# An attention and max-out kernel on one Trainium2 core: 84 steps at which the order of the main part departs from its own rule

## The chip, the core and the metric

The kernel runs on one core of one Trainium2 chip. The metric is the device time in microseconds (us) of one execution. Before the change its median over 10 runs is 330.27 us, from 329.93 to 330.78.

## What is computed

Cut to what matters, the reference is:

```python
# B, N, m, C = 4, 12544, 32, 128; d_ff = 1024
def mab(q, kv):                       # attention in which keys and values are the same rows
    s = (q @ kv.transpose(0, 2, 1)) / sqrt(C)
    a = exp(s - s.max(-1)); a /= a.sum(-1) + 1e-9
    return a @ kv
h = mab(inducing, x)                  # 32 inducing rows look at all of x: "pooling", h is 32 x 128 per batch
y = mab(x, h)                         # every row of x looks at the 32 rows of h
out = maximum(y @ w1, y @ w2) @ w_out # 50176 rows in all
```

The kernel uses max(a, b) = a + relu(b - a). With E the exponentials of the second attention (32 per row), it forms relu(E @ (h @ (w2 - w1))), multiplies it by w_out, adds the linear part E @ (h @ w1 @ w_out), and divides each row by the sum of its exponentials at the very end.

## The kernel before

The 50176 rows are cut into 392 chunks of 128 rows, 98 per batch. Sixteen chunks (four "quarters" of four) make a block. There are three kinds of work for TensorE, and they use the array in three shapes:

- A **phase** (L899, matmuls at L957) works in row tiles: four matmuls, one per quarter, each with 32 rows of the array and 512 output columns, side by side. Each fills one of the eight PSUM banks with the input of a relu. One of the four may be the linear part of a group ("L", four matmuls with 128 columns, written `ps<-m,e`). ScalarE (L973) or VectorE (L976) then evicts each relu bank into the `relu` tile; whichever the planner thinks will end sooner takes it. Every phase needs four free banks.
- A **final product** (L792 in `final_one`, L780) works with the whole array: one chunk's relu piece times one eighth of w_out, 128 columns. There are 3136 of them. Thirty-two make a group of four chunks, which VectorE scales into an output tile (L819 in `evict_group`) and SyncE's queue stores (L844). The sums of exponentials (L622 in `dens`) are small full-array matmuls.
- **Work in column tiles**: staging a block, which makes its E (`stage`, L582, evicted by ScalarE at L594), and, for the pooling of the next batch, its scores (`pool_scores`, L309, evicted at L320) and its accumulation (`pool_accum`, L357 and L370, added up by VectorE at L385). The scores need x transposed by DMA (L171), the accumulation needs the exponentials transposed by DMA (L346); both are issued on SyncE's queue, from `side_work`, by count of chunks done. The next batch's x is loaded by GpSimd's queue (L165) once the last accumulation of a batch has been summed (L391).

The order of the main part is not written out by hand and not left to a scheduler. A loop (L1097) makes it, one step at a time, while the program is built. It keeps a clock, `ck`, with estimates of when TensorE, ScalarE, VectorE and each bank come free. The next four phase jobs have a time `tp` at which the banks and the staged block are ready; the next final product has a time `tf` at which its relu piece is ready. The rule takes the phase if

```python
if tp < INF and lag() <= 128 + LIMIT and (tp <= ck.pe + early or tp <= tf and tf > ck.pe):
    if column_work(len(jobs) + 1):
        continue
    phase(jobs)
```

and otherwise the final product. `lag()` counts how far the phases are ahead. `column_work` looks just before a phase, or when the array is not in its full shape, for work in column tiles whose bank is free; it stages a block that is soon wanted, and it runs a pooling job if the array is already in column tiles, if two or more such jobs wait, or if the job is late. After the last step every engine has a fixed instruction list, with semaphores between engines; nothing is decided at run time.

Of the kernel before, what the change touches and what calls it, by code (L numbers as in the profile page):

```python
# [16 lines left out]
INF = 1e9  # L17
# [85 lines left out]
def kernel(  # L103
# [35 lines left out]
    ck = Clock()  # L139
# [57 lines left out]
    with tc.manual_schedule(engines={ET.PE, ET.DVE, ET.Activation, ET.Pool, ET.SP}):  # L197
# [313 lines left out]
        def weights_1b():  # L511
            for h in range(2):
                nc.gpsimd.tensor_sub(w21[:, 512 * h : 512 * (h + 1)], w_of[h][0], w_of[h][1])
# [16 lines left out]
        def weights_3():  # L530
            bi, ps = bank([128, 512])
            ck.wait(max(ck.bank[bi], w_of["w1T"]), "w")
            for jb in range(NJB):
                nc.tensor.matmul(
                    out=ps[:, 0:128],
                    lhsT=w1T[:, jb, :],
                    rhs=woutp[:, jb, :],
                    start=(jb == 0),
                    stop=(jb == NJB - 1),
                )  # L540
            end = ck.run(0.056 * NJB)
            nc.scalar.mul(out=w1out, in_=ps[:, 0:128], mul=-1.0)
            ck.bank[bi] = w_of["w1out"] = ck.on_act(end, 0.2)
# [303 lines left out]
        def finals_left():  # L847

            n = -state["mm"]
            for i in range(state["g"], state["lin"]):  # L850
                n += len(groups[i].chunks) * NJB
            return n

        def next_job(q):

            k, u = ptr[q]
            while k < len(blocks) and (q >= len(blocks[k].units) or u >= len(blocks[k].units[q])):
                k, u = k + 1, 0
            ptr[q] = [k, u]
            if k >= len(blocks):  # L860
                return None
            blk = blocks[k]
            if blk.staged is None:
                return None
            if relu_slot(blk, q) is None:
                return None
            return blk, blk.units[q][u]

        def want_linear():
            while state["lin"] < len(groups) and groups[state["lin"]].full:  # L870
                state["lin"] += 1
            if state["lin"] >= len(groups):
                return None
            g = groups[state["lin"]]
            if g.blk.staged is None or finals_left() > LINEAR_AHEAD:
                return None
            if st[g.blk.b].get("m1r", 0.0) > ck.pe + 0.2:
                return None
            return g

        LINEAR_AHEAD = 18
        LIMIT = -16

        def plan_phase(linear=True):
            jobs = []
            gl = want_linear() if linear else None
            for q in range(4):
                if gl is not None and gl.chunks[0][0] == q:
                    jobs.append(("L", q, gl, None))
                    continue  # L890
                j = next_job(q)
                if j is not None:
                    jobs.append(("U", q, j[0], j[1]))
            return jobs

        def lag():
            return 4 * state["issued"] - state["done"]
# [116 lines left out]
        def ready(f, a):  # L1014

            d = st[a[0]]
            now = ck.pe
            if f is pool_scores and a[1] >= NEU and ("eT", a[1] - NEU) not in d:
                return False
            if f is pool_turn and a[1] >= NEU and ("sum", a[1] - NEU) not in d:  # L1020
                return False
            if f is pool_scores:
                return d.get(("T", (U * a[1] + U - 1) // (P1 // 2)), INF) + 8.0 <= now
            if f is pool_rest:
                return d.get(("T", 13), INF) + 6.0 <= now
            if f is pool_turn:
                return d.get(("eu", a[1]), (0, INF))[1] <= now
            if f is pool_accum:
                return d.get(("eT", a[1]), (0, INF))[1] + 9.5 <= now and (a[1] < NU - 1 or "et" in d)
            if f is small_rep:  # L1030
                return d.get("esrr", INF) <= now
            if f is small_h:
                return d.get("haccr", INF) <= now
            if f in (small_hwd, small_m1):
                if f is small_m1 and a[0] == 0 and w_of["w1out"] > now:
                    return False
                return d.get("hT4r", INF) <= now
            return True
# [4 lines left out]
        def side_work():  # L1043
            while jobs_at and min(jobs_at) <= chunks_done[0]:
                pending.extend(jobs_at.pop(min(jobs_at)))
            for job in list(pending):
                f, a = job
                if f in COL or not ready(f, a):
                    continue
                if f in FULL:  # L1050
                    if min(ck.bank) > ck.pe + 0.1 or ck.mode != "full":
                        continue
                    pending.remove(job)
                    f(*a)
                    return
                pending.remove(job)
                f(*a)

        def column_work(banks):

            if sorted(ck.bank)[banks - 1] > ck.pe + 0.12:
                return False
            if want_stage(8 if chunks_done[0] > 14 else 3):
                stage(blocks[state["stage"]])
                state["stage"] += 1
                return True
            jobs = [job for job in pending if job[0] in COL and ready(*job)]
            late = jobs and (chunks_done[0] >= due[jobs[0]] + 8 or jobs[0][1][1] == NU - 1)
            if jobs and (ck.mode == "col" or len(jobs) > 1 or late):
                pending.remove(jobs[0])  # L1070
                f, a = jobs[0]
                f(*a)
                return True
            return False

        def want_stage(ahead):
            k0 = state["stage"]
            if k0 >= len(blocks):
                return False
            left = []  # L1080
            for q in range(4):
                next_job(q)
                k, u = ptr[q]
                left.append(sum(len(blk.units[q]) for blk in blocks[k:k0] if q < len(blk.units)) - u)
            free = k0 < NE2 or min(g.blk.index for g in groups[state["g"] :]) > k0 - NE2
            return min(left) <= ahead and free and all(
                "hT4" in st[qu.b] and "hwd" in st[qu.b] for qu in blocks[k0].quarters if qu
            )

        phase(plan_phase(False))  # L1090
        weights_3()
        phase(plan_phase(False))
# [1 line left out]
        state["stage"] = 2  # L1094
        weights_1b()
        START = ck.pe
        while state["g"] < len(groups) or held:  # L1097
            side_work()
            if held and ck.mode == "full":
                linear_last(0.0)  # L1100
            if ck.mode != "full" and column_work(1):
                continue
            if min(ck.bank) <= ck.pe + 0.1 and want_stage(1):
                stage(blocks[state["stage"]])
                state["stage"] += 1
                continue
            jobs = plan_phase()
            tp = INF
            tf = final_ready()
            useful = len(jobs) == 4 or jobs and (tf >= INF or state["stage"] == len(blocks) and lag() <= 48)  # L1110
            if useful and len(jobs) > 0:
                fr = sorted(ck.bank)[len(jobs) - 1]
                tp = max([fr - 0.095] + [(a.blk.staged if kind == "L" else a.staged) for kind, q, a, u in jobs])
            early = 0.2 if ck.mode == "col" else 0.0
            if tp < INF and lag() <= 128 + LIMIT and (tp <= ck.pe + early or tp <= tf and tf > ck.pe):
                if column_work(len(jobs) + 1):
                    continue
                phase(jobs)
            elif tf < INF:
                keep_busy(tf)  # L1120
                ck.wait(tf, "relu")
                final_one()
            elif tp < INF:
                phase(jobs)
            elif pending:
                f, a = pending.pop(0)
                f(*a)
            else:
                raise AssertionError(("stuck", state, ptr, chunks_done, jobs, pending[:3]))
        assert not pending and not jobs_at  # L1130


# [28 lines left out]
```

The softmax here doesn't subtract the row's maximum and nothing guards it: scores larger than these inputs give would overflow.

## Time and profile before

| | before |
|---|---|
| median of 10 runs | 330.27 us |
| the profiled execution | 329.93 us |
| its span, first to last instruction | 328.0 us |
| TensorE busy (PE) | 322.0 us, 98% |
| VectorE busy (DVE) | 285.3 us, 87% |
| ScalarE busy (ACT) | 280.6 us, 86% |
| GpSimd busy (POOL) | 25.8 us, 8% |
| share of TensorE in the chain that ended last | 96% |
| granted TensorE clock | 1.000 |
| DMA, mean over the span | 164 GB/s |

The profile is that of one execution of 329.93 us. Its span is 1.93 us shorter than its time, and the execution is the fastest of the ten, 0.34 us under the median. "Busy" counts an instruction from its start to its end; matmuls overlap, so a final product is shown with 220 ns though one follows the other every 56 ns. The distances between starts are therefore what counts on TensorE. Until about 25 us the kernel pools the first batch; the first final product starts at 25.6 us, the last at 324.4 us, and the stretch between is the main part that the loop orders.

### The profile page before, as it was taken

To read this page: it belongs to the slowest core of one execution; us is meant where nothing else is said; L and a number is where in the kernel's file an instruction comes from. 1 tells how busy PE (TensorE), PEld (TensorE's weight loads), DVE (VectorE), ACT (ScalarE), POOL (GpSimd) and SP (SyncE) were. 2 spreads that over 40 slices of the span, in tenths; PEclk is the share of its full clock that TensorE was granted. 3 is DMA by queue.
4 is the path that set the end of the run, shared out by engine and by line. 5 is a ranking of instruction groups with operands and counts; after the bars stand their busy time and mean duration, and the time that the engine had idled before them with its cause. 6 is when DMAs were issued, how large, how long until landed. Compare 5 with 4: busy or idle time off the path is not lost.

```text
span 328.0 us, 12601 instructions
## 1 busy us (share of the span) xinstructions
PE 322.0 (98%) x5401; PEld 243.7 (74%) x5401; DVE 285.3 (87%) x532; ACT 280.6 (86%) x562; POOL 25.8 (8%) x54
## 2 busy tenths in 40 slices
PE   7999999999999999999999999999999999999996
PEld 3886777777767777777787777777767777778785
DVE  3359999999989999998989999988989989989873
ACT  3689899998789899988888999998968999999961
POOL 7351030000310000000040000000000000000000
PEclk9999999999999999999999999999999999999999
DMA  8999999975299998672379999983212312222233
GB/s 207 207 206 214 285 239 183 194 205 163 58 232 243 238 234 187 171 155 95 125 147 243 232 254 206 194 181 100 103 61 98 114 67 99 98 98 98 82 115 113
DMA packets 70823, 53.65 MB, mean 164 GB/s; under 512 B 52176, under 2 KB 55408, under 8 KB 70768
## 3 DMA queue, kind: packets, MB, share of 16 engines
q1 hardware_dynamic: 64656, 38.63, 47.6%
q0 software_dynamic: 6112, 14.22, 22.1%
q8 instruction: 42, 0.69, 0.9%
q14 instruction: 13, 0.11, 0.1%
HBM read 28.33 MB, written 25.69 MB: 165 GB/s over the span
## 4 chain that ended last, share of the span: by engine, by line
PE 96%; DVE 1%; issue 1%; ACT 0%; DVEq 0%; ACTq 0%
PE ps L792 60%; PE ps L957 22%; PE ps L582 3%; PE ps L232 2%; PE ps L357 1%; PE ps L309 1%; PE ps L648 1%; PE ps L248 1%; PE ps L280 1%; PE ps L622 1%; DVE relu L976 1%; PE ps L749 1%; PE ps L271 1%; PE ps L640 0%; PE ps L464 0%
## 5 line engine op out<-in xcount | busy, mean ns | idle before, releaser
L973 ACT ACTIVATE relu<-ps 128x512 f16<-128x512 f32 x463 | 244.6, 604 | 31.1 <-PE ps L957 24.1
L976 DVE TENSOR_SCALAR relu<-ps 128x512 f16<-128x512 f32 x321 | 205.8, 681 | 18.8 <-PE ps L957 17.9
L792 PE MATMUL ps<-woutp,relu 128*128 128x128 f16 x3136 | 218.1, 220 | 0.0
L792 PEld LDWEIGHTS <-relu 128*128 128x128 f16 x3136 | 177.3, 98 | 39.4 <-issue 28.3
L957 PE MATMUL ps<-e,hwd 32*128 32x512 f16 (+2 forms) x880 | 89.0, 360 | 0.0
L819 DVE TENSOR_TENSOR o<-ps,rp 128x512 f32<-128x512 f32 (+3 forms) x108 | 68.6, 635 | 5.7 <-PE ps L792 3.1
L957 PEld LDWEIGHTS <-hwd 32*128 32x128 f16 x880 | 25.0, 91 | 21.1 <-issue 0.8
L957 PE MATMUL ps<-m,e 32*128 32x128 f16 x381 | 38.8, 217 | 0.0
L957 PEld LDWEIGHTS <-e 32*128 32x128 f16 x381 | 21.4, 92 | 2.6
L165 POOL DMA_DIRECT2D xn<-in_x_dram x31 | 16.8, 552 | 8.1 <-DMA xn<-in_x_dram 4.4
L236 DVE COPY xT<-ps 128x512 f16<-128x512 f16 (+3 forms) x11 | 5.5, 504 | 7.8 <-PE ps L232 7.7
L594 ACT ACTIVATE e<-ps 128x512 f16<-128x512 f32 (+2 forms) x21 | 11.6, 572 | 0.0
L320 ACT ACTIVATE eu<-ps 128x512 f16<-128x512 f32 x18 | 10.8, 619 | 0.0
L582 PE MATMUL ps<-xT,hT 128*32 128x512 f16 (+3 forms) x114 | 10.1, 366 | 0.0
L164 POOL COPY pace<-esr 128x1 f32<-128x1 f32 x2 | 0.4, 186 | 115.9 <-DVE esr L391 115.9
L239 ACT COPY xT<-ps 128x768 f16<-128x768 f16 (+3 forms) x11 | 6.1, 557 | 2.8 <-PE ps L232 2.6
L232 PE MATMUL ps<-identity,xn 128*128 128x128 f16 x98 | 7.4, 218 | 0.1
L582 PEld LDWEIGHTS <-hT 128*32 128x32 f16 x114 | 2.8, 93 | 5.7 <-issue 5.1
L257 ACT ACTIVATE et<-ps 128x448 f16<-128x448 f32 (+4 forms) x11 | 4.5, 413 | 2.6 <-PE ps L248 2.6
L632 DVE RECIPROCAL rp<-ps 128x16 f32<-128x16 f32 (+2 forms) x28 | 6.7, 239 | 0.0
L232 PEld LDWEIGHTS <-xn 128*128 128x128 f16 x98 | 5.6, 97 | 1.3 <-DVE xn L644 0.9
L622 PE MATMUL ps<-ones_q,e 128*128 128x4 f16 x102 | 6.5, 165 | 0.0
(96 smaller groups left out, 117.5 us busy)
## 6 DMA issues: line engine op xcount, KB each, us to landing
out_dram<-o SPq DMA_DIRECT2D x90, 256.0 KB, 2.5
xn<-in_x_dram POOLq DMA_DIRECT2D x24, 448.0 KB, 11.9
out_dram<-o SPq DMA_DIRECT2D x10, 128.0 KB, 3.1
xn<-in_moe_w_dram POOLq DMA_DIRECT2D x4, 256.0 KB, 14.2
xn<-in_x_dram POOLq DMA_DIRECT2D x4, 224.0 KB, 10.1
xT<-xn SPq DMA_TRANSPOSE x42, 4.0
xf<-in_x_dram SPq DMA_DIRECT2D x1, 512.0 KB, 3.6
xf<-in_x_dram SPq DMA_DIRECT2D x1, 384.0 KB, 4.1
```

The lines of the kernel that those rows point to most:

```text
L165: nc.gpsimd.dma_start(out=xn_at[b, i][:, 0:n, :], in_=xr[b, :, k0 : k0 + n, :])
L232: nc.tensor.transpose(ps[:, j, :], xn[:, g + j, :], identity16)
L320: nc.scalar.activation(out=eu, in_=ps, func=AF.Exp, scale=scale, accum_out=st[b]["es"][:, u : u + 1])
L582: nc.tensor.matmul(out=ps[32 * q : 32 * (q + 1), 128 * t : 128 * (t + n)], lhsT=hq, rhs=xT[:, c : c + n, :], start=True, stop=True, tile_p ...
L594: nc.scalar.activation(out=blk.e2[:, 0 : 128 * wd], in_=ps[:, 0 : 128 * wd], func=AF.Exp, scale=st[0]["rs"] if blk.b == 0 else scale,)
L622: nc.tensor.matmul(out=ps[:, 4 * t : 4 * t + 4], lhsT=blk.e2[:, 128 * t : 128 * (t + 1)], rhs=ones_q, start=True, stop=True,)
L632: nc.vector.reciprocal(out=blk.rp[:, 0:wd, :].rearrange("p t q -> p (t q)"), in_=ps[:, 0 : 4 * wd])
L792: nc.tensor.matmul(out=g.ps[:, 128 * c : 128 * (c + 1)], lhsT=g.blk.relu[q][:, 128 * (jb * w4 + t) : 128 * (jb * w4 + t + 1)], rhs=woutp[: ...
L819: nc.vector.tensor_mul(osb[:, 0:n, :], g.ps[:, 0 : n * C].rearrange("p (s c) -> p s c", s=n), rp)
L957: nc.tensor.matmul(**seq[i])
L973: nc.scalar.activation(out=dst, in_=src, func=AF.Relu)
L976: nc.vector.tensor_scalar(out=dst, in0=src, scalar1=0.0, scalar2=None, op0=ALU.max)
```

## The change

A table `DEV` lists 84 steps of the loop, and how the order departs from the rule there: 1 puts a phase off by one product, 2 takes a phase that would be ready within 0.2 us of the planner's clock, 3 does without column work at this step, 4 lets a single pooling job run when a phase is about to be taken. No instruction is added or removed: the loop makes the same products, phases, evictions, transfers and stores. The core of the diff (the table is cut):

```diff
+        DEV = {
+            0: 1, 27: 1, 32: 1, 35: 2, 52: 1, 87: 2, 157: 3, 168: 1, 169: 4, 181: 2, 244: 2, 247: 1, 397: 4,
...
+            3, 1625: 2, 1658: 3, 1723: 1, 1736: 3, 1739: 1, 1764: 1, 1777: 1, 1796: 4, 1801: 3, 1812: 1,
+            1843: 1, 1966: 3, 1981: 1, 1997: 1, 2021: 1
+        }
-        def column_work(banks):
+        def column_work(banks, soon=False):
...
-            if jobs and (ck.mode == "col" or len(jobs) > 1 or late):
+            if jobs and (soon or ck.mode == "col" or len(jobs) > 1 or late):
...
+        step = -1
         while state["g"] < len(groups) or held:
+            step += 1
+            how = DEV.get(step, 0)
...
-            if ck.mode != "full" and column_work(1):
+            if ck.mode != "full" and how != 3 and column_work(1):
                 continue
...
-            if tp < INF and lag() <= 128 + LIMIT and (tp <= ck.pe + early or tp <= tf and tf > ck.pe):
-                if column_work(len(jobs) + 1):
+            now = tp <= ck.pe + early or tp <= tf and tf > ck.pe
+            if how == 1 and tf < INF:
+                now = False
+            if how == 2 and tp <= ck.pe + 0.2:
+                now = True
+            if tp < INF and lag() <= 128 + LIMIT and now:
+                if how != 3 and column_work(len(jobs) + 1, how == 4):
                     continue
                 phase(jobs)
```

The numbers of the steps count rounds of the loop, 3418 in all; the table ends at step 2021, when 228 of the 392 chunks are done.

## The prediction

> **What bounds the kernel now.** I read the page's busy shares first, then the chain that ended last, then the groups of evictions, then stretches of the span, and last the timeline of TensorE where the order changes.
>
> ```profile
> PE 322.0 (98%) x5401; PEld 243.7 (74%) x5401; DVE 285.3 (87%) x532; ACT 280.6 (86%) x562; POOL 25.8 (8%) x54
> ...
> PE 96%; DVE 1%; issue 1%; ACT 0%; DVEq 0%; ACTq 0%
> ...
> L973 ACT ACTIVATE relu<-ps 128x512 f16<-128x512 f32 x463 | 244.6, 604 | 31.1 <-PE ps L957 24.1
> L976 DVE TENSOR_SCALAR relu<-ps 128x512 f16<-128x512 f32 x321 | 205.8, 681 | 18.8 <-PE ps L957 17.9
> ```
>
> TensorE carries 96% of the chain. ScalarE and VectorE have 31.1 and 18.8 us of idle time before their relu evictions, and most of it ends with a phase: they wait for TensorE, not it for them. Stretches say the same (columns: length, then busy time of PE, PEld, DVE, ACT, POOL):
>
> ```profile
> 25.60:60.00 34.40, 34.35 (x530) 24.75 (x529) 31.61 (x57) 32.75 (x66) 4.21 (x6) 1.00 1.11 225
> ...
> 180.00:210.00 30.00, 30.00 (x479) 22.42 (x476) 28.21 (x50) 27.77 (x56) 0.00 (x0) 1.00 1.08 215
> ```
>
> With the same instructions, only two things on TensorE can change: how often the array changes its shape, and how long it waits for a bank or a relu piece. The timeline prices both. Undisturbed (start, length, line):
>
> ```profile
> 123.89 0.39 PE L957 MATMUL ps<-e,hwd 32*128 32x512 f16 x4
> 124.22 0.95 PE L792 MATMUL ps<-woutp,relu 128*128 128x128 f16 x14
> 125.11 0.39 PE L957 MATMUL ps<-e,hwd 32*128 32x512 f16 x3
> ```
>
> From the phase to the products is 0.33 us; the four matmuls, side by side, take what one of 512 columns takes, 0.216 us (distance of two such full-array matmuls in the trace). The boundary of shapes is thus about 0.10 us. On the other side, 14 products at 56 ns are 0.78 us of the 0.89, and again 0.10 us is the boundary. The same where the loop has to wait:
>
> ```profile
> 31.50 0.40 PE L582 MATMUL ps<-xT,hT 128*32 128x512 f16 x4
> 31.83 0.45 PE L792 MATMUL ps<-woutp,relu 128*128 128x128 f16 x5
> 32.21 0.52 PE L957 MATMUL ps<-e,hwd 32*128 32x512 f16 x4
> 32.72 0.95 PE L792 MATMUL ps<-woutp,relu 128*128 128x128 f16 x14
> 33.61 0.54 PE L957 MATMUL ps<-e,hwd 32*128 32x512 f16 x4
> 34.09 0.40 PE L792 MATMUL ps<-woutp,relu 128*128 128x128 f16 x4
> ```
>
> These two phases take 0.51 and 0.48 us: 0.18 and 0.15 us went to banks that were not yet evicted. Over the whole main part, phases longer than the median of their form by over 0.04 us lose 1.1 us, and late products and jobs some 0.8 us more: 1.9 us is all that there is to win from waits. A pooling job alone, and two pairs of them in one visit:
>
> ```profile
> 69.29 0.40 PE L309 MATMUL ps<-xT,inducingT 128*32 128x512 f16 x4
> 69.62 0.45 PE L792 MATMUL ps<-woutp,relu 128*128 128x128 f16 x5
> ...
> 211.59 0.41 PE L357 MATMUL ps<-xn,eT 128*32 128x128 f16 x16
> 211.82 0.39 PE L309 MATMUL ps<-xT,inducingT 128*32 128x512 f16 x4
> 212.04 0.40 PE L357 MATMUL ps<-xn,eT 128*32 128x128 f16 x16
> 212.35 0.40 PE L309 MATMUL ps<-xT,inducingT 128*32 128x512 f16 x4
> 212.68 0.73 PE L792 MATMUL ps<-woutp,relu 128*128 128x128 f16 x10
> ```
>
> Alone, a job costs 0.33 us; as one more in a visit, 0.22 us (211.59 to 211.82). In the long visit the second pair has to wait for banks: its steps are 0.31 and 0.33 us, where a stream is 0.22 and stream and boundary are 0.32, so 0.1 us is lost.
>
> **The change, part by part.** First, what it does. Of the 84 entries nearly all ask for what the rule does anyway (a phase put off that was not due) or for what cannot be had (a phase or a job whose bank is not free). The loop with steps 35, 87, 1125, 1777 and 2021 alone gives the changed kernel's instruction order exactly. So there are two phases one or two products sooner (35 at 31 us, 87 at 36 us of the trace) and three a product later (at 128, 186 and 207 us). The rest is what follows from these in the planner's clock.
>
> *Removed work:* none. On each engine the counts are the same: 3136 products, 1261 phase matmuls, 13 filling matmuls (L749), 463 relu evictions on ScalarE and 321 on VectorE, 108 stores, 42 and 18 DMA transposes.
>
> *Boundaries.* In TensorE's order, full, row and column tiles change 485 times before and 482 times after. Two of the joins can be named: the last scores of batch 1, alone at 69.29, now follow a staging, and the two accumulations of batch 2 around 162 us (16 and 20 matmuls in two visits) become one of 36. In batch 3, scores that stood in pairs are spread over stagings that take place anyway. Three boundaries at 0.10 us: -0.3 us. [...]
>
> *Waits on banks and pieces.* To see them I laid the trace's own intervals along both orders: 56 ns a product, 216 ns a phase or column job, 0.10 us a boundary, evictions 0.48 us apart on ScalarE and 0.60 on VectorE (the trace's distances with the queue full), 0.05 us from an eviction's end to TensorE. Along the old order this gives 2.3 us of waiting between 24.7 us and the end (0.9 of it before the first changed step, in both orders alike). It comes to the last product 1.9 us sooner than the trace, mostly in the small products between batches, which stay. Along the new order it gives 1.8 us. Where: at 32.2 us the staging now stands two products sooner, so the phase behind it comes 2 x 0.056 = 0.11 us later after the phase before it, and about 0.1 of its 0.18 us goes; at 149.5 us the scores behind a staging find their bank 0.06 us nearer; at 211 and 224 us the double pairs are broken up, 0.19 us; some ten small ones of 0.01 to 0.05 us between 72 and 260 us, of both signs, give 0.15 us. Sum: -0.5 us. The bounds: a new order might bring as much waiting as it takes away, or more, +0.4; and it cannot take away more than about 1.0 of the 1.9 us, since the waits before 31 us and in the chains between batches (86 to 94, 239 to 246 us) stay where they are.
>
> *The other queues.* What is moved with the scores of batch 3 is their eviction (L320, 0.62 us, and 0.22 us for the row sum behind it) on ScalarE and the DMA transpose of their exponentials (L346) on SyncE's queue, which now goes ahead of some transposes of x (L171) and stores. Each transpose keeps that queue about 1.9 us, so a transpose of x may start that much later; the scores that read them have over 5 us to spare, except the first (below). The loads of x on GpSimd's queue start with the sum at L391, about 0.5 us sooner. The stores have six output tiles, that is some 16 us. I cost all this at nothing; the cover is these spare times.
>
> [...]
>
> Sum: -0.3 - 0.5 = -0.8 us. Against the profiled execution, 329.93 us (328.0 and 1.93 around it), that is 329.1. The median is 0.34 us higher, 330.27, and so the median after should be 329.5 us (-0.24%).
>
> **The rivals.** About 0.2%, or 0.66 us, is what a measurement of this kernel can tell from no change, so the forecast lies just beyond.
>
> *The waits come back elsewhere.* Banks are used the moment that they come free: half of the phases start within 0.7 us of an eviction of their bank, a tenth within about 0.1. A product more or less can make a new wait at any of them. Then only the boundaries count, or not even they: -0.6 to +0.3 us, 330.0 in the middle. For it: the gains are many and small, and the laid-out times are 1.9 us from the trace. Against it: that difference lies outside the changed places, and making all evictions 2 or 4% longer in the lay-out leaves the gain between 0.7 and 1.0.
>
> *More than forecast.* The trace loses more at 32.2 and 33.6 us (0.33) than the lay-out (0.2); if all such places go, -1.2 us, 329.1.
>
> *A transfer becomes the bound, slower.* The first scores of batch 3 move from 199.7 to about 194.4 us. They read the first 16 chunks of transposed x, whose third transpose lands at 191.2 us: 8.5 us to spare become 3.2. If this landing is later than 194.4, TensorE stands still with all that is queued behind it, since its order is fixed. The first pair of transposes took 9.5 us to land, against a median of 4.0. A landing 5 us late costs 1.8 us, and the sum is +1.0: 331.3. It decides from a delay of 4.7 us on (1.5 us of standing still). Against it: the loads start sooner, not later.
>
> **How the numbers follow.** Forecast, both terms: 0.50, between 329.0 and 329.6. Waits come back: 0.35, 329.6 to 330.6. More: 0.07. Slower by a transfer or a bank: 0.08. Faster by over 0.2% is the first and the third, 0.57; within it 0.35; slower 0.08. The range from 328.9 to 330.4 holds the first case, most of the second and part of the third.
>
> **What would show it.** Right: 482 boundaries still at 0.10 us each; the phase near 32.2 us under 0.45 us; no visit with L357, L309, L357, L309 at 211 us; the first final product at the same 25.6 us and the last about 0.8 us sooner than 324.4; the gain growing in small steps, 0.1 by 36 us, 0.2 by 80, 0.45 by 170, 0.8 by 260. Wrong: idle time of PE before L309 near 194 us ended by a DMA; phases over 0.5 us at new places; a last product at 324.2 or later.

## The result and the profile after

The median after is 329.43 us (15 runs, 328.99 to 329.93). The kernel before has 330.37 us over 51 runs (329.77 to 331.07), the ten of the table further up among them. The ratio is 0.9973, with a 95% interval from 0.9967 to 0.9979: faster by 0.27%, or 0.9 us, just beyond the 0.2% that can be told from no change.

A whole execution says little about where that comes from: the profiled one of the changed kernel took 329.82 us, its span 327.9 us, both only 0.1 below before. What serves is the time between the first and the last final product in the trace (L792), called "the stretch" from here. It is the part that the loop orders.

| kernel | first L792 | last L792 | stretch | profiled execution |
|---|---|---|---|---|
| before | 25.62 | 324.44 | 298.82 | 329.93 |
| after | 26.43 | 324.35 | 297.92 | 329.82 |

The stretch is 0.90 us shorter, and the medians differ by 0.94. The main part began 0.81 us later, which has nothing to do with the change (last section).

On the page, the rows that the prediction rested on have hardly moved:

```profile
PE 322.0 (98%) x5401; PEld 243.9 (74%) x5401; DVE 284.8 (87%) x532; ACT 280.9 (86%) x562; POOL 25.7 (8%) x54
...
PE 96%; DVE 1%; ACT 1%; issue 1%; DVEq 0%; ACTq 0%
...
L985 ACT ACTIVATE relu<-ps 128x512 f16<-128x512 f32 x463 | 244.8, 603 | 28.9 <-PE ps L969 20.6
L988 DVE TENSOR_SCALAR relu<-ps 128x512 f16<-128x512 f32 x321 | 205.6, 681 | 18.2 <-PE ps L969 17.3
```

The counts and the durations are the same, and TensorE still carries 96% of the chain. The evictions' idle time fell from 31.1 and 18.8 us to 28.9 and 18.2: a faster TensorE makes them wait less, and there is plenty left. The stretch from 180 to 210 us, with columns as before, shows how the same 30 us hold more matmuls, 497 for 479, with the clock at 1.00 again:

```profile
180.00:210.00 30.00, 30.00 (x497) 22.49 (x492) 28.01 (x49) 28.05 (x57) 0.00 (x0) 1.00 1.12 215
```

More matmuls in one window are work done sooner or other work; they are no gain by themselves. For that I compared the time, counted from the first final product, at which the same final product starts in both traces. After is ahead by 0.11 us from product 64 on (34.8 us), by 0.18 at product 512 (78 us), by 0.31 at 1408 (166 us), by 0.93 at 2432 (264 us), and by 0.90 at the end. So a third of the gain is there by 166 us, and most of the rest comes between 166 and 264 us.

The first changed steps, on TensorE's timeline (start, length, line; this whole execution runs 0.81 us behind that of before):

```profile
32.19 0.40 PE L582 MATMUL ps<-xT,hT 128*32 128x512 f16 x4
32.52 0.56 PE L792 MATMUL ps<-woutp,relu 128*128 128x128 f16 x7
33.02 0.41 PE L969 MATMUL ps<-e,hwd 32*128 32x512 f16 x4
33.42 0.95 PE L792 MATMUL ps<-woutp,relu 128*128 128x128 f16 x14
34.31 0.55 PE L969 MATMUL ps<-e,hwd 32*128 32x512 f16 x4
34.79 0.51 PE L792 MATMUL ps<-woutp,relu 128*128 128x128 f16 x6
```

Seven products and not five stand between the staging and the phase. From the phase to the next product it is 0.40 us now, before it was 0.51: of 0.18 us lost, 0.07 are left. The phase behind it still takes 0.48. And the double pairs of batch 3 are gone, as forecast. In the visit at 215 us L357 and L309 stand once each:

```profile
214.95 0.40 PE L582 MATMUL ps<-xT,hT 128*32 128x512 f16 x4
215.18 0.40 PE L357 MATMUL ps<-xn,eT 128*32 128x128 f16 x16
215.42 0.40 PE L309 MATMUL ps<-xT,inducingT 128*32 128x512 f16 x4
215.75 0.95 PE L792 MATMUL ps<-woutp,relu 128*128 128x128 f16 x14
```

Its last two steps, 0.24 and 0.33 us, are what a stream and what a stream with a boundary take, to 0.02 us. Before, 0.31 and 0.33 were seen in one visit.

### The profile page after: what moved, and what is told of

Same layout as the page of the kernel before. It is cut to its first block, busy times and chain, and to the rows that moved or that the text cites. A ratio compares the mean times of both kernels' runs of the same rounds, so it can differ in the third digit from the quotient of the medians.

```text
span 327.9 us, 12592 instructions
## 1 busy us (share of the span) xinstructions
PE 322.0 (98%) x5401; PEld 243.9 (74%) x5401; DVE 284.8 (87%) x532; ACT 280.9 (86%) x562; POOL 25.7 (8%) x54
## 4 chain that ended last, share of the span: by engine, by line
PE 96%; DVE 1%; ACT 1%; issue 1%; DVEq 0%; ACTq 0%
PE ps L792 60%; PE ps L969 22%; PE ps L582 3%; PE ps L232 2%; PE ps L357 1%; PE ps L309 1%; PE ps L648 1%; PE ps L248 1%; ACT relu L985 1%; DVE relu L988 1%; PE ps L280 1%; PE ps L622 1%; PE ps L640 1%; PE ps L749 1%; PE ps L271 1%
## 5 line engine op out<-in xcount | busy, mean ns | idle before, releaser
L985 ACT ACTIVATE relu<-ps 128x512 f16<-128x512 f32 x463 | 244.8, 603 | 28.9 <-PE ps L969 20.6
L988 DVE TENSOR_SCALAR relu<-ps 128x512 f16<-128x512 f32 x321 | 205.6, 681 | 18.2 <-PE ps L969 17.3
L792 PE MATMUL ps<-woutp,relu 128*128 128x128 f16 x3136 | 218.1, 220 | 0.0
L792 PEld LDWEIGHTS <-relu 128*128 128x128 f16 x3136 | 177.2, 98 | 40.5 <-issue 30.1
L969 PEld LDWEIGHTS <-e 32*128 32x128 f16 x381 | 21.4, 92 | 2.6
```

The lines of the kernel that those rows point to most:

```text
L792: nc.tensor.matmul(out=g.ps[:, 128 * c : 128 * (c + 1)], lhsT=g.blk.relu[q][:, 128 * (jb * w4 + t) : 128 * (jb * w4 + t + 1)], rhs=woutp[: ...
L969: nc.tensor.matmul(**seq[i])
L985: nc.scalar.activation(out=dst, in_=src, func=AF.Relu)
L988: nc.vector.tensor_scalar(out=dst, in0=src, scalar1=0.0, scalar2=None, op0=ALU.max)
```

## The experiments

### The five steps alone

If 79 of the 84 entries are inert, a table with five entries is the changed kernel. (In this and the next edits the line stands in place of the whole table; the lines it replaces are not shown.)

```diff
+        DEV = {35: 2, 87: 2, 1125: 1, 1777: 1, 2021: 1}
```

> The table holds steps 35, 87, 1125, 1777 and 2021 alone: the instruction order is that of the changed kernel. If the other 79 entries do nothing, the time is that of the changed kernel, a ratio of 0.997 to 0.998, and the stretch from the first to the last final product is 297.9 us again, within 0.05, if this stretch is fixed by the order. If the stretch varies from one execution to the next by what was gained, it is anywhere between 297.5 and 298.8.

Measured: median 329.24 us against 330.39, ratio 0.9967 (0.9955 to 0.9980), stretch 297.92 us, the same as after to the hundredth. The five steps are the change.

### The five in three parts

Early, middle and late, each alone on the kernel before:

```diff
+        DEV = {35: 2, 87: 2}
```

> The table holds steps 35 and 87 alone; the order until about 85 us of the trace is that of the changed kernel, and after it that of the kernel before. One boundary of shapes fewer (484). Theory A (boundaries at 0.10 us and waits on banks both count, as in the prediction): -0.10 for the boundary and -0.13 for waits, -0.24 us between the first and the last final product. Theory B (only the boundaries count; the waits come back elsewhere): -0.10 us. In the median of the runs either lies within what can be told, 330.0 to 330.3; the two traces tell them apart.

```diff
+        DEV = {1125: 1}
```

> The table holds step 1125 alone; the order differs from the kernel before only between about 128 and 169 us. One boundary fewer (484). Theory A: -0.10 for the boundary and -0.10 for waits, -0.20 us between the first and the last final product. Theory B: -0.10 us.

```diff
+        DEV = {1777: 1, 2021: 1}
```

> The table holds steps 1777 and 2021 alone; the order differs from the kernel before only between about 186 and 296 us. One boundary fewer (484). Theory A: -0.10 for the boundary and -0.26 for waits (double pairs of pooling jobs broken up), -0.36 us between the first and the last final product. Theory B: -0.10 us. If the parts are independent, the three gains add up to that of the whole change, -0.90 us between the two traces.

| part | median, that of before | ratio (95%) | stretch | against before |
|---|---|---|---|---|
| early | 330.23, 330.18 | 0.9997 (0.9988 to 1.0005) | 298.65 | -0.17 |
| middle | 330.21 | 0.9995 (0.9984 to 1.0006) | 298.71 | -0.11 |
| late | 330.06 | 0.9999 (0.9990 to 1.0008) | 298.58 | -0.24 |

The medians can't tell any part from no change; the stretches can. The early and middle parts give in isolation what after shows at the same places. The late part does not: in after, the steps 1777 and 2021 are worth 0.59 us, alone only 0.24. The three make 0.52 of 0.90, so either the parts are not additive, or this run lost something of its own. Run once more:

> Steps 1777 and 2021 alone, once more. In the first profile the stretch from first to last final product was 0.24 us shorter than before, because one phase at 271.8 us of that trace lost 0.38 us to a VectorE eviction that started late with nothing to wait for in the profile. If that was of this one execution, the stretch is now 298.23 us (0.59 shorter than before), and the three parts add up to the whole change. If it belongs to the order, it is 298.58 again, and the parts do not add up.

It came out at 329.86 us with a stretch of 298.59, 0.23 less than before: the loss is no accident of one execution. The traces show where it is. From about 170 us on, the late part and after have the same instructions on every engine, and yet at 271 us they part. VectorE and TensorE of the late part (the bracket is idle time and what ended it):

```profile
270.29 0.63 DVE L987 TENSOR_SCALAR relu<-ps 128x512 f16<-128x512 f32 x1
271.49 1.29 DVE L987 TENSOR_SCALAR relu<-ps 128x512 f16<-128x512 f32 x2 [0.58 <-PE ps L792]
```

```profile
270.62 0.40 PE L968 MATMUL ps<-e,hwd 32*128 32x512 f16 x4
271.83 0.78 PE L968 MATMUL ps<-e,hwd 32*128 32x512 f16 x4
272.54 0.95 PE L792 MATMUL ps<-woutp,relu 128*128 128x128 f16 x14
```

and of the changed kernel at the same instructions:

```profile
270.78 0.63 DVE L988 TENSOR_SCALAR relu<-ps 128x512 f16<-128x512 f32 x1
271.64 1.29 DVE L988 TENSOR_SCALAR relu<-ps 128x512 f16<-128x512 f32 x2 [0.23 <-PE ps L969]
```

```profile
272.33 0.43 PE L969 MATMUL ps<-e,hwd 32*128 32x512 f16 x4
272.69 0.95 PE L792 MATMUL ps<-woutp,relu 128*128 128x128 f16 x14
```

The eviction starts 1.20 us after the one before it, where in after it is 0.86. Its bank had long been filled: TensorE's phase ended by 271.02, so VectorE started 0.47 us behind it, where in after it is 0.13 (271.64 less 271.51). TensorE, and ScalarE beside it, are at the same distances in both traces up to here. So VectorE stood still for 0.34 us too long, and the phase at 271.83 pays for it: 0.71 us to the products, in after 0.36. In the second run of the same kernel the delay is there again, 0.37 us.

### The stray delay moved

The same place in the work, with the same instructions on both sides, is late in one kernel and not in the other; but it is not the same place in VectorE's instruction stream, which is four entries longer in the late part (691 in the trace for 687) because of what differs before 170 us. So I put twelve small VectorE instructions at the start, which move everything after them along in that stream:

```diff
+        pad = consts.tile([128, 1], F32, name="pad")
+        for _ in range(12):
+            nc.vector.memset(pad, 0.0)
```

on the late part, on after and on before.

> Steps 1777 and 2021 alone, as in the two runs before, with twelve small VectorE memsets of an unused tile at the start of the kernel, where VectorE waits for x. In both profiles of that order one VectorE eviction, always the same, started 0.45 us late at 271.5 us, though all that it waits for had long ended, and from about 170 us on its instruction list is that of the changed kernel, where the same eviction is 0.1 us late. If the delay comes from where VectorE's instruction stream stands (its instructions are fetched in blocks of 8 KB, and one such packet follows within 1 us), the memsets move it elsewhere or away: the stretch between first and last final product falls from 298.58 to 298.23 us. If it comes from the order or the data, nothing changes: 298.58.

> The changed kernel with the same twelve memsets at the start. If the place in VectorE's stream decides, a delay of up to 0.45 us may appear at another eviction, and the stretch is between 297.92 and 298.3 us; otherwise it is 297.92 again.

> The kernel before with the same twelve memsets. The stretch is 298.82 us, or up to 0.45 us more or less if the place in VectorE's stream decides, for the kernel before may hold such a delay that was counted as a wait on a bank.

| twelve memsets on | one run | stretch | against before |
|---|---|---|---|
| late part | 329.58 | 298.24 | -0.58 |
| after | 329.50 | 297.93 | -0.89 |
| before | 330.20 | 298.84 | +0.02 |

In the padded late part the eviction and the phase are where they should be:

```profile
271.26 1.29 DVE L990 TENSOR_SCALAR relu<-ps 128x512 f16<-128x512 f32 x2 [0.23 <-PE ps L971]
```

```profile
271.95 0.43 PE L971 MATMUL ps<-e,hwd 32*128 32x512 f16 x4
272.31 0.95 PE L795 MATMUL ps<-woutp,relu 128*128 128x128 f16 x14
```

The late steps are thus worth 0.58 us, the three parts add up to -0.17 - 0.11 - 0.58 = -0.86 us, against -0.90 for all five, and before and after have no such delay to lose. That the delay comes back in a second execution and goes with twelve instructions far ahead of it fits a delay that hangs on a place in VectorE's instruction stream. It is not more than that: the padded late part ran once, and the memsets also bring a tile of their own and a start 0.1 us later, which no run here separates from them. What happens there is open, too. An instruction queue in the trace carries a packet of 8 KB behind the delay, at 272.17 and 272.15 us in the two runs, and with the memsets it comes at 265.92, so it follows VectorE's stream. In the traces of before and after such a packet starts at 270.29 and 272.90 us, behind 576 and 575 entries of VectorE's stream, while ScalarE's stands at 559 and 566. But in the late part it begins 0.7 us after the late eviction has started, and after has its packet without such a delay. That a fetch of code is the cause is not shown.

### The price of a boundary

The forecast counted three boundaries at 0.10 us; many more of them in one kernel show what one costs. In the kernel before, every twentieth product between the 2350th and the 3110th, if the array was in its full shape and in the midst of a group, got one small matmul in row tiles ahead of it. `warm` holds zeros (L213), so the result stays the same.

```diff
+            if 2350 <= state["done"] <= 3110 and state["done"] % 20 == 10 and state["mm"] and ck.mode == "full":
+                nc.tensor.matmul(
+                    out=g.ps[:, 0:128], lhsT=warm[32 * q : 32 * q + 32, 0:128], rhs=warm[32 * q : 32 * q + 32, 0:128],
+                    start=False, stop=False, tile_position=(32 * q, 0), skip_group_check=True,
+                )
```

> The kernel before, with 34 matmuls of zeros in a row tile put between final products from about 258 us on (128 columns, added onto the open group, so that nothing changes in the result); the planner's clock does not know of them, and the order is otherwise that of before. Each adds two boundaries of shapes (553 in place of 485) and a stream of 0.056 us. If a boundary costs 0.10 us: 34 x (0.20 + 0.056) = 8.7 us more. [...]

Measured: 339.26 us, ratio 1.0271 (1.0250 to 1.0291), stretch 307.75, 8.93 us more. There are 34 such matmuls, 0.263 us each. The matmul itself has 128 columns as a product has, and if it takes the 0.056 us from one product to the next, two boundaries share the other 0.207: an estimate of 0.103 us each, against the forecast's 0.10. Hardly any waiting can hide in the pauses: in the trace of before, steps behind 258 us lose 0.03 us to waits. On the timeline (L797 are the products here, L792 the small matmul):

```profile
262.78 0.79 PE L797 MATMUL ps<-woutp,relu 128*128 128x128 f16 x11
263.50 0.23 PE L792 MATMUL ps<-warm 32*128 32x128 f16 x1
263.65 0.28 PE L797 MATMUL ps<-woutp,relu 128*128 128x128 f16 x2
```

Eleven products are 0.62 us of the 0.72 up to 263.50: 0.10 for the boundary, and 0.15 - 0.056 = 0.09 for the way back.

### Waits without boundaries

If only boundaries counted, an order with the same 485 of them would run like before. Taking every phase up to 0.2 us sooner gives such an order, but phases then come to banks that are not yet evicted (the table of this run is written here as one expression):

```diff
+        DEV = {s: 2 for s in range(3500)}
```

> Every phase is taken as soon as it would be ready within 0.2 us (2 at all steps), where the change does that at two places. The boundaries stay at 485. Theory B (only boundaries count): no change, 330.3. Theory A, and the rival that waits come back: with the trace's intervals laid along this order, phases wait 6.9 us for banks in place of 2.3, so about 4.3 us slower, 334.5.

Measured: 334.38 us, ratio 1.0124 (1.0106 to 1.0142), stretch 4.16 us longer. The laid-out order had said 4.3. Steps that take over 0.02 us more than the shortest of their kind lose some 6.2 us in this trace and 2.0 in that of before, which is the 4.2 us. One of the many places:

```profile
104.82 0.40 PE L582 MATMUL ps<-xT,hT 128*32 128x512 f16 x4
105.15 0.45 PE L792 MATMUL ps<-woutp,relu 128*128 128x128 f16 x5
105.53 0.65 PE L968 MATMUL ps<-e,hwd 32*128 32x512 f16 x4
106.11 1.01 PE L792 MATMUL ps<-woutp,relu 128*128 128x128 f16 x15
```

From the phase to the product 0.58 us, of which 0.25 is a bank. Boundaries alone explain nothing here, for their count is the same, and the lay-out of intervals foresaw the size.

### An order that should be better

Eleven steps chosen by the same lay-out, with 482 boundaries as in after:

```diff
+        DEV = {87: 2, 1777: 1, 2021: 1, 1150: 1, 835: 2, 2107: 1, 2374: 1, 1193: 1, 531: 1, 952: 2, 20: 2}
```

> Another table, of eleven steps (20, 87, 835, 952: 2; 531, 1150, 1193, 1777, 2021, 2107, 2374: 1), chosen so that the trace's intervals laid along its order give the least waiting: 1.5 us, where the order before gives 2.3 and the changed one 1.8. Its boundaries are 482, as in the changed kernel. Theory A: 1.1 us less than before, 329.2, and 0.3 us less than the changed kernel between the first and the last final product (297.6). Theory B: as the changed kernel.

Measured: 329.14 us, ratio 0.9966 (0.9957 to 0.9975), stretch 297.81: 1.01 less than before and 0.11 less than after, where 0.3 less was hoped for. More than that difference went here (VectorE, then TensorE):

```profile
242.28 1.19 DVE L495 CAST m1bd<-ps 32x128 f16<-32x128 f32 x4
243.48 0.29 DVE L495 CAST m<-ps 128x128 f16<-128x128 f32 x1
```

```profile
243.44 0.75 PE L968 MATMUL ps<-e,hwd 32*128 32x512 f16 x4
244.13 0.90 PE L792 MATMUL ps<-woutp,relu 128*128 128x128 f16 x13
```

Five small copies between batches (L495) keep VectorE from 242.28 to 243.77. Three matmuls of the phase start at 243.44 or 243.45, but the fourth starts at 243.82, 0.05 us after the last copy has ended, and so the phase takes 0.69 us to the next product instead of 0.33. As a kernel it has the smallest stretch of all; by the medians (329.14 and 329.24 for the five steps) it can't be told from after.

## Why the prediction was right

The forecast for the median was 329.5 us, and it is 329.43; for the stretch -0.8, and it is -0.90.

**What bounds it: right.** All that changed is on TensorE; the other queues cost nothing: the waits that after's trace lists for its matmuls (L648, L271, L248 and L401: 1.2, 0.3, 0.3 and 0.2 us) end with VectorE or ScalarE, none with a DMA. Nor did the evictions become the bound: there is idle time left in front of them (28.9 and 18.2 us).

**Boundaries, -0.3: right.** In the traces' orders there are 485 before and 482 after, and the price is 0.103 us, estimated from the run with 68 more of them (8.93 us).

**Waits, -0.5: right in sum, -0.60, but not in where, and so in part by luck.** The measured gain without the boundaries is 0.90 - 0.30. The places that were named gave 0.26 us of the 0.35 forecast for them: at 32.2 us 0.11 (0.1), at 149.5 us 0.06 (0.06), at 211 and 224 us 0.09 (0.19). The two largest other terms were not in the forecast. That the waits "in the chains between batches (86 to 94, 239 to 246 us) stay where they are" is false for the second: the last accumulations come at other times against them, and that is the largest gain. Before and after on TensorE, with the repetition of the sums (L401) and the phases at 246 us:

```profile
238.30 0.55 PE L792 MATMUL ps<-woutp,relu 128*128 128x128 f16 x7
239.17 0.35 PE L401 MATMUL ps<-esr,repd 128*128 128x1 f32 x2 [0.32 <-DVE esr L391]
...
245.98 0.38 PE L957 MATMUL ps<-e,hwd 32*128 32x512 f16 x1
...
246.56 0.96 PE L792 MATMUL ps<-woutp,relu 128*128 128x128 f16 x14
```

```profile
239.62 0.23 PE L792 MATMUL ps<-woutp,relu 128*128 128x128 f16 x1
239.98 0.35 PE L401 MATMUL ps<-esr,repd 128*128 128x1 f32 x2
...
245.19 0.38 PE L969 MATMUL ps<-e,hwd 32*128 32x512 f16 x1
...
245.52 0.90 PE L792 MATMUL ps<-woutp,relu 128*128 128x128 f16 x13
```

Seven products end their streaming at 238.69, so L401 waited 0.48 us; in after it is 239.98 less 239.68, or 0.30. The phase of 245.98 takes 0.58 us to the products, its counterpart in after 0.33. That is 0.43 us. In before this phase waits for banks that VectorE frees. One of its four parts starts only at 246.24, 0.05 us after VectorE has ended this instruction, not far behind the small copies between batches (L495):

```profile
245.94 0.25 DVE L632 RECIPROCAL rp<-ps 128x16 f32<-128x16 f32 x1
...
246.24 0.39 PE L957 MATMUL ps<-e,hwd 32*128 32x128 f16 x2
```

The late part alone has the gain at both places too. In the other direction, the chain of batch 2 lost 0.16 us:

```profile
163.69 0.23 PE L792 MATMUL ps<-woutp,relu 128*128 128x128 f16 x1
164.00 0.35 PE L401 MATMUL ps<-esr,repd 128*128 128x1 f32 x2
```

```profile
164.08 0.23 PE L792 MATMUL ps<-woutp,relu 128*128 128x128 f16 x1
164.55 0.35 PE L401 MATMUL ps<-esr,repd 128*128 128x1 f32 x2 [0.25 <-DVE esr L391]
```

With 0.056 us for the product, L401 waited 0.25 us in before and 0.41 in after, and the middle part alone shows the same. Its last accumulation is now joined with another, which the forecast had counted as a saved boundary only; the phase just ahead of it gives 0.07 us back. Small waits of both signs make the rest. Counted over all steps that take over 0.02 us more than the shortest of their kind, waits fall from some 2.0 to 1.6 us; what is missing to 0.60 is in smaller differences.

**The gain in steps.** 0.1 by 36 us and 0.2 by 80 came out (0.11, 0.18). 0.45 by 170 was 0.31, mostly by the loss at 164 us. 0.8 by 260 was 0.93, by the gain at 239 to 246.

**Inert entries: right**, by the run with five.

**The rivals.** Waits that come back elsewhere are a real mechanism: the eager order loses 4.16 us by it, the chosen eleven steps a third of a microsecond, and after itself 0.16 us at 164 and 0.09 us at a phase at 73.97, where before had lost 0.08 us at 75.92. They did not eat the gain, and no phase over 0.5 us stands at a new place. "More than forecast" rested on the phase at 33.6 us, which kept all of its 0.15 us. The forecast's 1.9 us for a transpose on SyncE's queue is in the trace of before as the distance of starts with a store between (187.88, 189.80, 191.79 us); its own instruction takes 1.28 us in the median. The transfer stayed hidden: the scores of batch 3 start at 195.36 us (near the 194.4 forecast, with the late start of this execution) right behind the staging, 0.23 us after it, and nothing in the row ends with a DMA:

```profile
195.13 0.40 PE L582 MATMUL ps<-xT,hT 128*32 128x512 f16 x4
195.36 0.39 PE L309 MATMUL ps<-xT,inducingT 128*32 128x512 f16 x4
195.68 0.79 PE L792 MATMUL ps<-woutp,relu 128*128 128x128 f16 x11
```

**What failed of the signs.** "The first final product at the same 25.6 us" was 26.43, and the last came 0.09 us sooner, not 0.8. By the forecast's own sign, "a last product at 324.2 or later", this trace would have told against it; the median did not. The sign took the start of the main part for fixed, and it is not.

## What to carry to other kernels

When one engine is busy to 98% and the lists are fixed, price each kind of boundary and each wait from the distances of starts in the trace, and lay those intervals along both orders: it gave -0.8 for -0.9, in part by luck, -1.1 for -1.01, and +4.3 for +4.16. Take the chains between stages into that lay-out and don't assume that they stand still: both large errors of the forecast were there, and so was that of the eleven steps. And compare the same instruction in two traces, counted from a common point, before comparing spans: it shows 0.02 us where whole runs spread over 1 us.

## What the runs showed of the hardware

**The start varies by 0.9 us.** The code ahead of the first final product does the same transposes in every kernel here, and over 13 profiles it starts between 25.60 and 26.50 us. The slow start of after and the quick one of before:

```profile
5.18 1.03 PE L232 MATMUL ps<-identity,xn 128*128 128x128 f16 x8
6.01 1.04 PE L640 MATMUL ps<-warm 128*128 128x512 f16 x2
```

```profile
5.19 0.62 PE L232 MATMUL ps<-identity,xn 128*128 128x128 f16 x8
5.64 0.59 PE L640 MATMUL ps<-warm 128*128 128x512 f16 x2
```

The same matmuls take nearly twice as long, for about 2 us, and the change of their pace falls on the start of the trace's record of the granted clock. That record has its first entry, at full clock, at 6.90 us in after and at 5.00 us in before. Nothing is recorded ahead of it, which the page counts as full, so that it shows 1.000 for both. The distances of starts show it: up to that entry, matmuls of 512 columns follow each other every 427 ns and the transposes every 107 ns, behind it every 216 and 56 ns. In the profile of the early part the entry, at 5.82 us, falls among the eight transposes: up to 5.83 us they are 107 ns apart, from then on 56. Over the 13 profiles the entry lies between 4.3 and 6.9 us. It moves from one execution to the next, 1.9 us between before and after; what sets it is not shown.

This does not make every late start. In after with the memsets (26.09 us) the eight transposes follow each other at 56 ns, but at 21.4 us TensorE is idle for 0.46 us until VectorE has worked on the weights w1. How much of the 1.3 us over which runs of one kernel spread comes from the start is not shown.

**A fixed order is very exact.** The stretch of the same order repeats to 0.02 us: 297.92, 297.92 and 297.93 for after's three, 298.58 and 298.59 for the late part, 298.82 and 298.84 for before. (The third of after and the second of before are those with the memsets.)

**An engine can stand still without a cause in the trace.** VectorE started one eviction 0.34 and 0.37 us too late with its work ready, in both executions of one kernel, and not when twelve instructions were put in at the start.
